# Half of the channel products of an attention-and-mixing kernel end by ScalarE's maximum with zero and an adding transfer by GpSimd

## The chip, the cores and the metric

The kernel runs on one core of a Trainium2 chip. The metric is the device time of one execution in microseconds (us), from the program's start to its end; the median of several runs is compared. The engines are named as in the profile: PE is TensorE, PEld its weight loads, DVE is VectorE, ACT is ScalarE, POOL is GpSimd and SP is SyncE, which issues transfers.

## The reference

Eight batches, each with eight heads, 576 positions and a head size of 64. Attention keeps only the scores within `tau` of the row's maximum; its output is laid out as `x` (576 by 512 for each batch) and goes through a mixing layer:

```python
scores = scale * q @ k.T
scores = where(scores >= max(scores) - tau, scores, -1e9)
x = softmax(scores) @ v                       # heads side by side: 576 x 512
theta = x @ w_theta
y = w_tok_r @ (x * cos(theta)) + w_tok_i @ (x * sin(theta))
u = x + y
out = u + maximum(u @ w_ch, 0)
```

## The kernel before

Work goes in 32 pairs of heads (four pairs a batch). A pair has five units. A unit's scores are matmuls (L761) into PSUM banks. DVE reads them out with a running minimum of the negated scores, which is the maximum (L782, tile `sc`), ACT takes the exponential (L815, tile `s`), and DVE zeroes what lies under the threshold and sums the row (L822). The weights are then turned: in three pairs of four by DVE's transpose (L837), in the last pair of each batch by PE (L855), with ACT copying each turned block out of PSUM (L861, L873, tile `a`). The product with the values is L891, or L920 in the pairs turned by PE. ACT copies it into the tile `xT`, which holds one pair's 128 channels of `x` in fp32 as 128 by 576, and it is divided by the row sums (L969 on POOL, L975 on DVE).

Every fp32 operand of a matmul is split into a high part, rounded by ACT (L982 for `x`, L708 for `q`, L722 for `k`), and a low part, which is a subtraction on POOL or DVE (`low`, L539). Matmuls of 128 by 128 weights on 288 columns then build the products from three terms.

`mixture(b)` does the mixing layer of one batch while the attention of the next one runs. For each of four blocks of 128 channels `m` it makes the angle product (L1021; ACT writes the tile `ang` at L1041 and L1055), sines, the turned parts `zh` and `zl`, and the token product (L1209), which DVE adds onto `xT` at L1221. Then `xT` holds `u`. `parts_of` splits `u`, and the channel product of block `m` (again L1021, from weights `wm` that SP loads at L680) fills two banks, one for each half `h` of 288 columns. `evict` (L1255) ends it: one DVE instruction for each half takes the maximum with zero of the bank, adds `u` and writes onto `xT` (L1270). SP then stores `xT` (L1278).

The tile class `ang` has two buffers and `xT` has seven. A table of numbers, `ORDER`, names every operation of the program in the order in which it is issued, and so sets each engine's queue; `PLACES` names the buffer of each tile. Engines work through their queues in order, and a waiting instruction holds back those behind it. SP's transfers are in the same way in order of issue.

`evict` of before holds a second way, not taken there since `rc` and `rc0` are 0: for `m` under `rc`, and for all batches but the last, ACT writes the maximum into an `ang` tile and POOL adds it onto `xT`.

Of the kernel before, what the change touches and what calls it, by code (L numbers as in the profile page):

```python
# [79 lines left out]
        "4456744475625423500000040000004000044607650506740743067473236547236454575624376627535473625473"  # L80
# [45 lines left out]
        "0101010101010101010101010101010101010101010101010101010101010101"  # L126
    ),
    "zh4": (
        "0123012301230123012301230123012301230123012301230123012301230123"
    ),  # L130
    "zl4": (
        "0123012301230123012301230123012301230123012301230123012301230123"
# [296 lines left out]
def tile_attn_moe(  # L429
# [98 lines left out]
    def gps(occ, fn, key, R, W, lock=True):  # L528
        return op(POOL, occ, fn, key, R, W, tail=0.05, lock=lock)
# [856 lines left out]
```

## Time and profile before

| | |
|---|---|
| time, median of 3 runs | 952.08 us (949.31 to 953.31) |
| the profiled execution's own time | 950.14 us |
| its span, first to last instruction | 948.3 us |
| outside the span | 1.8 us |
| granted TensorE clock, mean over the span | 0.994 of full speed |

The profile is of one execution. Busy time of an engine is the time in which one of its instructions ran; a matmul's end is modelled, so that a busy PE may still hold short gaps. A line such as `A <- B` in the waits says that the engine of A sat idle until B had ended. "issue" stands for idle time with no releaser in the profile.

### The profile page before, as it was taken

The page shows a single profiled execution, that of the slowest core. Times are in us where ns is not written, and L with a number is a line of the kernel's source. Part 1 is how long each engine was busy: PE and PEld are TensorE (multiplying, and loading weights), DVE is VectorE, ACT ScalarE, POOL GpSimd, SP SyncE. Part 2 cuts the span into 40 slices and gives each one's busy share as a digit, 9 for nine tenths or more (in the row PEclk, how much of TensorE's full clock was granted, in tenths as well). Part 3 has the DMA queues.
Part 4 walks back from the last instruction along what each step waited for, and adds up shares of the span by engine and source line. Part 5 has one row for each costly group of instructions (what it writes and reads, how often), then busy time and mean ns, then how long its engine had stood idle before and what let it go on. Part 6 is the DMA issues. An engine that isn't in the chain of part 4 may idle for free.

```text
span 948.3 us, 30033 instructions
## 1 busy us (share of the span) xinstructions
PE 904.9 (95%) x12532; PEld 801.8 (85%) x12532; DVE 796.5 (84%) x1838; ACT 634.1 (67%) x1296; POOL 342.8 (36%) x390
## 2 busy tenths in 40 slices
PE   6889999999999999999899999999999999999998
PEld 5667788898898889888798988898898988899798
DVE  7999899979988988889798897879998798986342
ACT  7899997458945777467764767548784578635650
POOL 2234453125624345234432533432442353404110
PEclk9999999999999999999999999999999999999999
DMA  6366253435322353325403453044533153222322
GB/s 219 125 195 199 85 184 125 142 123 192 122 86 92 116 178 120 127 78 179 147 37 104 136 192 112 4 172 122 192 99 112 55 196 123 70 97 98 114 70 73
DMA packets 59288, 118.80 MB, mean 125 GB/s; under 512 B 19441, under 2 KB 28561, under 8 KB 56593
## 3 DMA queue, kind: packets, MB, share of 16 engines
q1 hardware_dynamic: 59008, 116.89, 37.2%
q8 instruction: 98, 1.61, 0.7%
q14 instruction: 38, 0.30, 0.1%
q10 hardware_dynamic: 144, 0.00, 0.0%
HBM read 103.09 MB, written 13.78 MB: 123 GB/s over the span
## 4 chain that ended last, share of the span: by engine, by line
PE 60%; DVE 22%; ACT 10%; issue 5%; POOL 2%; DMA 0%; SPq 0%; DVEq 0%; ACTq 0%; POOLq 0%
PE banks_ps__66 L1209 19%; PE banks_ps__66 L1021 12%; PE banks_ps__66 L761 10%; PE banks_ps__66 L891 9%; DVE sc L782 6%; DVE s L822 6%; PE banks_ps__66 L855 4%; DVE a L837 4%; PE banks_ps__66 L1164 3%; PE banks_ps__66 L920 2%; ACT s L815 2%; POOL z L1139 1%; DVE xl L539 1%; DVE z L1089 1%; ACT L1117 1%
## 5 line engine op out<-in xcount | busy, mean ns | idle before, releaser
L815 ACT ACTIVATE s<-sc,nm 128x576 f32<-128x576 f32 x288 | 219.5, 777 | 73.0 <-DVE sc L782 57.3
L822 DVE SCALAR_TENSOR_TENSOR s<-sc,nm,s 128x576 f32<-128x576 f32 x288 | 249.7, 888 | 14.9 <-ACT s L815 7.9
L782 DVE TENSOR_SCALAR_CACHE_REDUCE sc<-banks_ps__66 128x576 f32<-128x576 f32 x261 | 188.3, 744 | 23.0 <-PE banks_ps__66 L761 21.7
L761 PE MATMUL banks_ps__66<-k,q 64*128 64x288 f32 (+1 forms) x1728 | 173.9, 313 | 12.9 <-DVE sc L782 7.9
L1021 PE MATMUL banks_ps__66<-xh,wm 128*128 128x288 f32 x1024 | 170.9, 304 | 2.2 <-issue 1.6
L761 PEld LDWEIGHTS banks_ps__66<-k,q 64*128 64x128 f32 (+1 forms) x1728 | 137.9, 189 | 39.8 <-issue 15.2
L1209 PE MATMUL banks_ps__66<-wt_h,zh 128*128 128x288 f32 x576 | 159.1, 303 | 1.3 <-ACT zh L1170 0.4
L1209 PE MATMUL banks_ps__66<-wt_l,zh 128*128 128x288 f32 x576 | 158.0, 299 | 0.0
L1021 PEld LDWEIGHTS banks_ps__66<-xh,wm 128*128 128x128 f32 x1024 | 144.8, 190 | 9.5 <-issue 6.2
L1139 POOL TENSOR_TENSOR z<-z,xT 128x288 f32<-128x288 f32 x112 | 98.7, 914 | 128.6 <-ACT z L1120 118.0
L837 DVE STREAM_TRANSPOSE a<-s 128x576 f32<-128x576 f32 x160 | 117.4, 757 | 20.6 <-PE banks_ps__66 L891 18.6
L539 POOL TENSOR_TENSOR xl<-xT,xh 128x288 fp32r<-128x288 f32 x78 | 75.3, 987 | 141.8 <-ACT xh L982 120.5
L891 PE MATMUL banks_ps__66<-a,v 32*64 32x144 f32 x5760 | 105.9, 286 | 12.9 <-issue 11.0
L1209 PEld LDWEIGHTS banks_ps__66<-wt_h,zh 128*128 128x128 f32 x576 | 106.8, 188 | 7.0 <-issue 4.1
L891 PEld LDWEIGHTS banks_ps__66<-a,v 32*64 32x64 f32 x5760 | 91.5, 130 | 23.5 <-issue 18.9
L1209 PEld LDWEIGHTS banks_ps__66<-wt_l,zh 128*128 128x128 f32 x576 | 107.3, 188 | 2.0 <-issue 1.9
L539 POOL TENSOR_TENSOR k<-rawk,k 128x288 fp32r<-128x288 f32 x62 | 57.9, 942 | 113.7 <-ACT k L722 78.1
L1209 PE MATMUL banks_ps__66<-wt_h,zl 128*128 128x288 f32 x576 | 98.7, 299 | 0.0
L539 POOL TENSOR_TENSOR q<-rawq,q 128x320 fp32r<-128x320 f32 x56 | 57.8, 1045 | 111.8 <-ACT q L708 111.8
L1021 PE MATMUL banks_ps__66<-xl,wm 128*128 128x288 f32 x512 | 92.6, 301 | 0.9 <-DVE xl L539 0.6
L1209 PEld LDWEIGHTS banks_ps__66<-wt_h,zl 128*128 128x128 f32 x576 | 82.8, 188 | 1.4 <-issue 1.2
L855 PE MATMUL banks_ps__66<-ident,s 128*128 128x128 f32 (+1 forms) x492 | 74.8, 284 | 3.1 <-DVE s L822 2.1
(84 smaller groups left out, 1275.0 us busy)
## 6 DMA issues: line engine op xcount, KB each, us to landing
wm<-wm_dram SPq DMA_DIRECT2D x64, 512.0 KB
v<-in_vp_dram SPq DMA_DIRECT2D x20, 1152.0 KB
rawq<-in_qT_dram SPq DMA_DIRECT2D x31, 320.0 KB
rawk<-in_kT_dram SPq DMA_DIRECT2D x31, 288.0 KB
out_dram<-xT SPq DMA_DIRECT2D x31, 288.0 KB
rb<-sums_dram SPq DMA_DIRECT2D x64, 128.0 KB
v<-in_vp_dram SPq DMA_DIRECT2D x12, 576.0 KB
z<-in_w_tok_dram SPq DMA_DIRECT2D x9, 576.0 KB
```

The source lines that it names most:

```text
L539: eng.tensor_tensor(out=out()[:, c0:c1], in0=in0()[:, c0:c1], in1=in1()[:, c0:c1], op=ALU.subtract)
L761: nc.tensor.matmul(ps()[:, 2 * j + h, :HS], q[a]()[r, i * P : (i + 1) * P], k[c]()[r, h * HS : (h + 1) * HS], start=(x == 0), stop=(x == 2),)
L782: lambda j=j, sc=sc, scaled=scaled: nc.vector.tensor_scalar(out=sc().rearrange("p (a b) -> p a b", a=2), in0=ps()[:, 2 * j : 2 * j + 2, :H ...
L815: lambda j=j, sc=sc, weights=weights: nc.scalar.activation(out=weights(), in_=keys(sc()), func=AF.Exp, bias=nm()[:, j : j + 1], scale=-1.0),
L822: lambda j=j, sc=sc, total=total, weights=weights: nc.vector.scalar_tensor_tensor(out=weights(), in0=keys(sc()), scalar=nm()[:, 2 + j : 3 ...
L837: nc.vector.transpose(out=a()[:, :, j, 32 * i : 32 * i + 32], in_=src.rearrange("p (c q) -> p c q", q=32))
L855: nc.tensor.transpose(out=tp()[: k1 - k0, c * P : (c + 1) * P], in_=flat()[:, k0:k1], identity=ident)
L891: nc.tensor.matmul(ps()[64 * h : 64 * h + 64, b, :w], v()[r, c, h, :], a()[r, c, h, :], start=(c == 0), stop=(c == 17))
L1021: nc.tensor.matmul(ps[h]()[:, :HS], wm()[:, a, c, :], parts[c][bb]()[:, h * HS : (h + 1) * HS], start=first and n == 0, stop=final and n = ...
L1139: eng.tensor_tensor(out=zi, in0=zi, in1=x[m]()[:, c0:c1], op=ALU.mult)
L1164: nc.tensor.transpose(out=tp()[:, i * P : (i + 1) * P], in_=z()[:, c : c + P], identity=ident)
L1209: nc.tensor.matmul(ps()[:, :HS], zz[c][lo]()[:, zz[c][2]], w[:, c, hs], start=(q + n == 0), stop=(q + n == len(work) - 1),)
```

## The change

For blocks `m` = 0 and 1 of batches 0 to 6 (`rc` and `rc0` are now 2), that is for 14 of the 32 channel products, the second way of `evict` is taken, with another last step. ACT writes the maximum with zero of each half into an `ang` tile (two instructions a block, 28 in all, L1269 of the kernel after). After the second half one transfer issued by GpSimd adds the tile of 128 by 576 onto `xT` in SBUF (`add_to`, 14 in all, L538). The 28 DVE instructions of L1270 for these blocks are gone; 36 stay. The store of `xT` by SP waits for the transfer's landing.

`low` gets a parameter `by_dma` that no caller sets. `ORDER` is a new table throughout, and the buffers of `zh4`, `zl4` and `ang` follow it.

```diff
-    "pad_pe": 0.12, "pad_dve": 0.021, "pad_act": 0.148, "rc": 0, "za": 0, "zq": 0, "ab0": 0, "rc0": 0, "za0": 0, "zq0": 0,
+    "pad_pe": 0.12, "pad_dve": 0.021, "pad_act": 0.148, "rc": 2, "za": 0, "zq": 0, "ab0": 0, "rc0": 2, "za0": 0, "zq0": 0,
...
 ORDER = (
-    "176 3 -9 3 75 -71 -176 177 2 -153 144 10 -9 79 -251 183 -169 160 -134 135 -122 131 146 -145 2 -1 3 8 -9 -186 "
...
+    "179 -3 -6 3 -172 26 150 71 -77 9 -8 -158 164 3 -181 174 9 68 -198 122 9 146 -290 145 2 -1 3 8 -9 -186 188 -187 "
...
+    def add_to(out, src, key, R, W, kb):
+        o = gps(0.87, lambda: nc.gpsimd.dma_start(out=out(), in_=src(), accum_op=ALU.add), key, R, W, lock=False)
+        o.kb = 1.2 * kb
+
...
                         c_act(HS, True), lambda: nc.scalar.activation(out=part()[:, hs], in_=ps()[:, :HS], func=AF.Relu), key,
                         (ps,), ((part, h),),
                     )
-                    gps(
-                        c_pool(HS),
-                        lambda: nc.gpsimd.tensor_tensor(out=x[m]()[:, hs], in0=part()[:, hs], in1=x[m]()[:, hs], op=ALU.add),
-                        key, ((part, h), x[m]), ((x[m], [0, 1, ("h", h)]),),
-                    )
+                    if h:
+                        add_to(lambda: x[m](), lambda: part(), key, (part, x[m]), ((x[m], [0, 1, ("h", 0), ("h", 1)]),), 288)
                     return
```

Where the program's queues changed is shown at one place, the channel products of batch 4. Line numbers of the kernel after are higher: L1277 there is L1270 of before, L792 is L782, L832 is L822, L825 is L815, L871 is L861, L803 is L793, L544 is L539, L979 is L969, L709 is L699, L731 is L721, L690 is L680, L747 is L737, L960 is L950 and L1285 is L1278.

DVE, before, from the first end of block 0 to the second end of block 1 (`s_` and a number is one unit's weights):

```order
L1270 SCALAR_TENSOR_TENSOR xT<-banks_ps__66,xT 128x288
L822 SCALAR_TENSOR_TENSOR s_9834,rows<-sc,nm,s_9834 128x9x64
L1270 SCALAR_TENSOR_TENSOR xT<-banks_ps__66,xT 128x288
L782 TENSOR_SCALAR sc,nm<-banks_ps__66 128x576 x2
L822 SCALAR_TENSOR_TENSOR s_9834,rows<-sc,nm,s_9834 128x9x64
L782 TENSOR_SCALAR sc,nm<-banks_ps__66 128x576
L822 SCALAR_TENSOR_TENSOR s_9882,rows<-sc,nm,s_9882 128x9x64 x2
L822 SCALAR_TENSOR_TENSOR s_9921,rows<-sc,nm,s_9921 128x576
L1270 SCALAR_TENSOR_TENSOR xT<-banks_ps__66,xT 128x288
```

DVE, after, the same units (9834 and 9882 are now called 9852 and 9893):

```order
L832 SCALAR_TENSOR_TENSOR s_9852,rows<-sc,nm,s_9852 128x9x64
L792 TENSOR_SCALAR sc,nm<-banks_ps__66 128x576 x2
L832 SCALAR_TENSOR_TENSOR s_9852,rows<-sc,nm,s_9852 128x9x64
L792 TENSOR_SCALAR sc,nm<-banks_ps__66 128x576
L832 SCALAR_TENSOR_TENSOR s_9893,rows<-sc,nm,s_9893 128x9x64 x2
L832 SCALAR_TENSOR_TENSOR s_9929,rows<-sc,nm,s_9929 128x576
```

The ends of the blocks have left the queue, and what stood between them is in the same order as before.

ACT, before, the same stretch:

```order
L815 ACTIVATE s_9834<-sc,nm 128x9x64
L861 COPY a<-banks_ps__66 128x4x128
L815 ACTIVATE s_9882<-sc,nm 128x9x64
L861 COPY a<-banks_ps__66 128x4x128
L815 ACTIVATE s_9882<-sc,nm 128x9x64
L793 ACTIVATE nm<-nm,small 128x2
```

ACT, after:

```order
L825 ACTIVATE s_9852<-sc,nm 128x9x64
L1269 ACTIVATE ang<-banks_ps__66 128x288
L825 ACTIVATE s_9893<-sc,nm 128x9x64
L1269 ACTIVATE ang<-banks_ps__66 128x288
L871 COPY a<-banks_ps__66 128x4x128
L803 ACTIVATE nm<-nm,small 128x2
L825 ACTIVATE s_9893<-sc,nm 128x9x64
```

The two maxima of block 0 now stand between the exponentials; one copy (L861) has moved behind them and the small L793 ahead of the last exponential, and no work has left the stretch.

SP, after, from the store of block 0 (the first row) to that of block 1 (the last):

```order
L1285 DMA out_dram<-xT 128x576
L747 DMA v<-in_vp_dram 128x2304
L731 DMA rawk<-in_kT_dram 128x576
L690 DMA wm<-wm_dram 128x1024 x2
L747 DMA v<-in_vp_dram 128x2304
L960 DMA sums_dram<-rt 9x128
L709 DMA rawq<-in_qT_dram 128x640
L1285 DMA out_dram<-xT 128x576
```

Behind each store, which now waits for an adding transfer, stand loads of the next pairs.

## Rows read from the trace of the kernel before

**Rows 1.** Page, part 1: busy us of each engine (share of the span), instructions.

```profile
PE 904.9 (95%) x12532; PEld 801.8 (85%) x12532; DVE 796.5 (84%) x1838; ACT 634.1 (67%) x1296; POOL 342.8 (36%) x390
```

**Rows 2.** Busy us of each engine by stage; first the stage and its length.

```profile
0.00:75.00 75.00, 59.39 (x495) 44.08 (x495) 68.92 (x180) 63.09 (x132) 21.01 (x34) 0.95 0.58 182
75.00:875.00 800.00, 777.16 (x11492) 692.79 (x11491) 699.72 (x1607) 543.10 (x1111) 312.47 (x344) 1.00 0.37 123
875.00:948.30 73.30, 68.37 (x550) 64.97 (x549) 27.82 (x52) 27.95 (x55) 9.34 (x12) 1.00 0.26 90
```

**Rows 3.** Waits of PE from 75 to 875 us: us in total, times, longest.

```profile
PE banks_ps__66 L891 <- issue: 11.0, 9, 2.0
...
PE banks_ps__66 L761 <- DVE sc L782: 1.3, 4, 0.4
PE banks_ps__66 L855 <- DVE s L822: 1.1, 4, 0.3
```

**Rows 4.** Groups by line and form: busy us, mean ns of one, idle before.

```profile
L1270 DVE SCALAR_TENSOR_TENSOR xT<-banks_ps__66,xT 128x288 f32<-128x288 f32 x64 | 27.9, 450 | 16.8 <-PE banks_ps__66 L1021 13.9 <-PE banks_ps__66 L855 2.0 <-ACT xh L982 0.5
...
L1041 ACT ACTIVATE ang<-banks_ps__66 128x288 f32<-128x288 f32 x64 | 25.8, 415 | 12.7 <-PE banks_ps__66 L1021 7.3 <-DVE z L1089 5.1 <-PE banks_ps__66 L946 0.2
```

**Rows 5.** Stages (columns PE, PEld, DVE, ACT, POOL) around blocks 0 and 1.

```profile
199.00:205.00 6.00, 6.00 (x135) 5.29 (x135) 2.73 (x7) 2.11 (x7) 0.00 (x0) 1.00 0.48 162
312.60:322.00 9.40, 9.40 (x86) 8.71 (x84) 8.65 (x23) 8.79 (x21) 2.90 (x4) 1.00 0.60 184
421.00:432.00 11.00, 11.00 (x101) 9.99 (x100) 9.46 (x29) 10.80 (x25) 3.32 (x5) 1.00 0.35 103
533.00:542.00 9.00, 9.00 (x81) 8.44 (x78) 8.62 (x26) 8.46 (x20) 2.41 (x3) 1.00 0.59 198
644.50:657.00 12.50, 12.50 (x112) 11.45 (x111) 11.65 (x35) 12.17 (x29) 4.87 (x6) 1.00 0.34 89
756.40:766.20 9.80, 9.80 (x86) 8.93 (x86) 8.80 (x27) 9.69 (x25) 4.84 (x6) 1.00 0.42 145
867.80:874.00 6.20, 6.20 (x52) 6.18 (x51) 4.32 (x14) 3.22 (x9) 0.00 (x0) 1.00 0.66 224
...
sum 51.70, PE 51.70 PEld 47.52 DVE 47.17 ACT 49.91 POOL 18.34; mean PE 10.34 PEld 9.50 DVE 9.43 ACT 9.98 POOL 3.67
```

**Rows 6.** Sum of the stages 322:338, 432:450, 542:558, 657:672 and 766.2:782.

```profile
sum 80.80, PE 80.35 PEld 66.29 DVE 77.93 ACT 52.30 POOL 34.48; mean PE 16.07 PEld 13.26 DVE 15.59 ACT 10.46 POOL 6.90
```

**Rows 7.** DVE's instructions of L1270 in one stage: length, busy us, count.

```profile
644.50:657.00 12.50, 1.81 (x4) 1.00 0.34 89
```

**Rows 8.** Chain of waits from 644 to 672 us: start, length, what.

```profile
653.21 0.79 ACT s L815
...
655.13 0.68 ACT s L815
...
657.83 0.69 ACT s L815
...
661.47 0.37 DVE xT L1270
```

**Rows 9.** Instructions of L539: ns least/median/most, first and last start.

```profile
L539 POOL TENSOR_TENSOR xl<-xT,xh x78: 794/812/1397, 110.6 to 932.3; 128x288 fp32r<-128x288 f32 x78
...
L539 DVE TENSOR_TENSOR xl<-xT,xh x25: 708/986/1421, 112.8 to 933.5; 128x576 fp32r<-128x576 f32 x25
```

**Rows 10.** Waits of SP's queue: us in total, times, longest.

```profile
SPq L1278 <- DVE xT L1270: 37.3, 11, 9.7
...
SPq L958 <- DMA sums_dram<-rt: 24.7, 18, 3.9
```

**Rows 11.** Issues of the stores by SP: ns least/median/most of one issue.

```profile
L1278 SPq DMA_DIRECT2D out_dram<-xT x31: 332/382/1504, 199.9 to 942.8; - x31
```

More of the change, by code (lines that the diff above doesn't have):

```diff
@@ L79 @@
         "60074446576565447457764665756457746577456700000040000007000074504570505640664055006744567564574676564765"
-        "4456744475625423500000040000004000044607650506740743067473236547236454575624376627535473625473"
+        "4456744475625423500000040000004000044607650506740743067473236547236454575624373627535473625473"
     ),
@@ L125 @@
     "ang": (
-        "0101010101010101010101010101010101010101010101010101010101010101"
+        "010101010101010101010101010101010101010101010101010101010101010101010101010101"
     ),
     "zh4": (
-        "0123012301230123012301230123012301230123012301230123012301230123"
+        "0123012301230123012301230123012301230123012301230123012301230112"
     ),
     "zl4": (
-        "0123012301230123012301230123012301230123012301230123012301230123"
+        "0123012301230123012301230123012301230123012301230123013201230121"
     ),
@@ L534, in load, with low @@
         return o
-    def low(on_pool, out, in0, in1, key, R, W, n=S):
+    def add_to(out, src, key, R, W, kb):
+        o = gps(0.87, lambda: nc.gpsimd.dma_start(out=out(), in_=src(), accum_op=ALU.add), key, R, W, lock=False)
+        o.kb = 1.2 * kb
+    def low(on_pool, out, in0, in1, key, R, W, n=S, by_dma=False):
         def go(eng, c0=0, c1=n):
@@ L541, in low @@
         (b, p), k = W, AT["cut"]
+        if on_pool and by_dma:
+            both = (b, [(p, i) for i in range(k)])
+            act(c_act(n), lambda: nc.scalar.activation(out=out(), in_=in0(), func=AF.Copy, scale=-1.0), key, R[:1], (both,))
+            add_to(lambda: out().bitcast(F32), in0, key, R[:1], (both,), n // 2)
+            return
         if on_pool:
```

321 rows, old and new, of the table ORDER are left out of this document.

## The prediction

> **What bounds the kernel now.** I read the page's busy times first. PE is busy for 904.9 of 948.3 us, DVE for 796.5, ACT for 634.1 [rows 1]. The view by stage then splits the span: in the first 75 us PE is idle for 15.6 us, in the 800 us from 75 to 875 for 22.8 us, and in the last 73 us, where DVE has little left, for 4.9 us [rows 2]. So the middle is PE's, to 97%. Who ends PE's idle time there: half of it (11.0 us) has no releaser and lies in the products with the values, and each wait for DVE is about 1 us in total [rows 3]. DVE is busy for 87% of the middle, close behind PE, and has to be looked at by stretch.
>
> The change touches 28 places, four a batch in batches 0 to 6. I laid a window around the four of each batch, from the end of the first half of block 0 to that of the last half of block 1 [rows 5]; in batch 0 the last of the four comes later. The reader is to see three things. PE is busy for every hundredth of a microsecond in all seven. In batches 1 to 5 both other engines are packed: of 51.70 us DVE works 47.17 and ACT 49.91, so ACT, not DVE, is the fuller one. In batches 0 and 6 DVE and ACT both have gaps. The reason for ACT's load is in the code: these are the units of the pair that PE turns and whose turned blocks ACT copies. In the windows right behind (80.80 us in five batches) it is the other way round: DVE works 77.93 us, ACT only 52.30, and PE 80.35 [rows 6].
>
> **The change part by part.**
>
> Removed from DVE: 28 instructions of 450 ns [rows 4], 12.6 us. Batches 0 and 6 hold 8 of them, in windows with DVE idle: worth nothing. The other 20 are 9.0 us, 1.8 us a batch (batch 4 is shown in [rows 7]). PE has no idle time beside them, so PE's work covers them; what can be won is that DVE goes into its packed second window 1.8 us earlier.
>
> Added to ACT: 28 instructions. The nearest row is the same engine reading the same 288 columns of a bank into `ang`, 415 ns [rows 4]: 11.6 us in all, 1.66 us a batch. In the five full windows ACT's gaps are 51.70 - 49.91 = 1.79 us, 0.36 us a batch. So 1.3 us of ACT's work a batch is pushed into the second window, which has 28.5 us of ACT's time free. Until then exponentials and copies run up to 1.3 us late, and behind them wait DVE's L822 and then PE's transposes. In batch 4 the chain runs just there through ACT's exponentials, and from 658.5 us on through DVE [rows 8].
>
> The two together: from above, ACT is on the path each time and nothing is given back, 5 x 1.66 = +8.3 us. From below, DVE's head start goes through each time, -9.0 us. I take 0, for two reasons: PE, which covers both windows, has 0.45 us of idle time in 132.5 us [rows 5, 6], and ACT gives back in the second window what it lost in the first.
>
> Added to POOL: 14 issues. No row shows an issue by POOL. The nearest from below is an issue by SP, 0.38 us at the median [rows 11], from above the longest POOL subtraction, 1.40 us [rows 9]: 5 to 20 us on an engine that is busy for 36% of the span. POOL's idle time covers it, 33.4 us of the 51.7 [rows 5], and I cost it at nothing; without that cover it would come onto the splits of `x`, `q` and `k`. An issue also might hold up a DVE instruction. DVE's own subtraction L539 takes 708 ns at best, 986 at the median and 1421 at worst, while POOL works beside it with a spread of 794 to 1397 [rows 9]. 14 x 0.28 is 3.9 us, 14 x 0.71 is 9.9 us, and none is zero; I take zero, as an issue reads and writes far fewer bytes than such a subtraction and is nearer to SP's issues.
>
> The Trainium skill, "SBUF — State Buffer", section "SBUF: two separate sides", speaks against the change: a transfer issued by GpSimd has its descriptors written by GpSimd, which is locked out of SBUF while DVE runs in a mode that uses both ports, so that the transfer lands late. The rows above do show DVE and POOL getting in each other's way; no row here shows it for an issue. The page tells of a transfer of 0.62 us that took 3.1 us beside such an instruction; 2.5 us more would leave the landing below within what SP bears, so by that rule the sum would stay, and it is the third rival that hangs on it.
>
> The adding transfer itself: 295 KB are read twice and written once. No row has one. In the window at 867.8 us all transfers together move 224 GB/s [rows 5]; one pass of 295 KB at that rate is 1.3 us, two are 2.6 us, and twice that when the windows' transfers share the rate: 2.6 to 5.3 us, estimates. The longest wait for the landing of a small transfer (9 by 128 row sums) was 3.9 us [rows 10]. I take 4 to 6 us. What waits for it is the store on SP, and behind that the loads of `v`, `rawk` and `wm`. SP already stands up to 9.7 us at the stores, 37.3 us in total [rows 10], while PE loses nothing to loads in the middle. So this is covered up to about 10 us. The `ang` tile is needed again only by the next batch's angles, behind blocks 2 and 3.
>
> The new order: the whole table is new, and queues differ slightly far from the 28 places too. What a new order can give back is PE's idle time, at most 22.8 us in the middle [rows 2]; what it can cost has no such bound. There is no reason in the rows for either sign. I take 0 and a width of 6 us.
>
> **Sum.** 950.14 us of the profiled execution (span 948.3 and 1.8 around it) - 0 + 0 = 950.1 us. This execution lies 1.9 us under the median of 952.08 and inside its runs (949.31 to 953.31), so the same sum from the median is 952.1. I say **951 us**: no change that a measurement here can tell, since about 0.5% (4.8 us) is needed for that, under 947.3 or over 956.8 us.
>
> **The rivals.**
>
> 1. DVE's head start counts, faster. For it: DVE is 96% busy in the second windows [rows 6], and in batch 4 the chain from 658.5 us on is DVE's [rows 8]; ACT has room there, and a new order can use that. Against it: PE is busy throughout. The price is between half and all of the 9.0 us: 950.1 - 4.5 to - 9.0, 941 to 945.6 us.
>
> 2. ACT takes DVE's place, slower. The place is the five full windows: exponentials late by the four maxima, then L822, then the transposes and PE's product with the values. For it: ACT's 97% there against DVE's 91% [rows 5], and the rows of ACT's queue, where the maxima stand between exponentials. Against it: PE has other work queued. It decides as soon as PE runs dry in the 80 us behind, that is when its idle time there is no longer 0.45 us [rows 6]. Full price 950.1 + 8.3 = 958.4 us.
>
> 3. The adding transfer lands late (DVE keeps POOL from its descriptors, or the transfer is slow), slower. It decides from a landing of about 10 us, the wait that SP bears now [rows 10]; at 15 us SP would be 5 us behind 14 times, and if one time in seven a load were late by that, 2 x 5 = 10 us: 960 us. Against it: transfers use 37% of their engines in the middle [rows 2].
>
> 4. The change doesn't do what it says: DVE's work only moves and the 9 us reappear as longer L822 beside POOL's issues. That is 950 us too, and counts with the forecast.
>
> **How the numbers follow.** Forecast with rival 4: 0.46, its own range 945 to 957, of which 0.05 falls under 947.3 and 0.04 over 956.8. Rival 1: 0.28, with 0.26 under 947.3. Rival 2: 0.18, of which 0.02 stays within the bound. Rival 3: 0.08. Faster is 0.05 + 0.26 = 0.31; within the bound 0.37 + 0.02 + 0.02 = 0.41; slower 0.04 + 0.16 + 0.08 = 0.28. The range that leaves out a tenth on each side goes from the middle of rival 1 to rival 2 and part of rival 3: 942 to 961 us.
>
> **What would show it.** In the profile after: L1270's successor 36 times instead of 64, DVE's busy time down by about 12 us, ACT's up by about 11.6 us with a new group of 28 at about 415 ns, and PE's busy time about as before (905 us). If the forecast holds, PE's idle time from 75 to 875 us is 18 to 28 us. Rival 1 shows as PE idle time under 18 us with waits of ACT for DVE (`sc`) shorter. Rival 2 shows as new waits of DVE for ACT's exponentials, or of PE for ACT's copies. Rival 3 shows as waits of SP for the adding transfer over 10 us, and POOL or PE behind loads. I am wrong if the time is outside 947 to 957 us, and wrong in the mechanism if PE's idle time moves by over 6 us while the time does not.

## The result and the profile after

The kernel after takes 959.46 us (median of 4 runs, 957.51 to 960.52), before in the same comparison 951.71 us: a ratio of 1.0100, interval 1.0075 to 1.0124. (The two medians alone give 1.0081, 7.75 us; the ratio on record is a little higher, and the medians' value lies inside its interval.) It is slower, against a forecast of no change. The profiled execution took 957.51 us, its span is 955.7 us, its mean granted clock 0.993. Line numbers are those of the order rows above: L832 is L822 of before, and so on.

Part 1 of the page of the kernel after, busy us of each engine, answers to [rows 1]:

```profile
PE 907.2 (95%) x12532; PEld 803.0 (84%) x12532; DVE 795.9 (83%) x1810; ACT 640.8 (67%) x1324; POOL 356.6 (37%) x404
```

DVE has 28 instructions fewer, but is busy for only 0.6 us less, where 12.6 us were taken from it. The stages answer to [rows 2] (columns PE, PEld, DVE, ACT, POOL, clock, DMA share, GB/s):

```profile
0.00:75.00 75.00, 59.94 (x490) 43.91 (x490) 68.01 (x178) 62.09 (x129) 19.85 (x34) 0.95 0.58 181
75.00:875.00 800.00, 772.04 (x11441) 687.49 (x11442) 697.52 (x1575) 545.66 (x1128) 325.20 (x356) 1.00 0.40 126
875.00:955.70 80.70, 75.23 (x603) 71.57 (x602) 30.34 (x60) 33.06 (x69) 11.59 (x14) 1.00 0.34 107
```

PE's idle time in the middle went from 22.8 to 28.0 us, and the last stage is 7.4 us longer: attention reaches 875 us with more work left. PE's waits in the middle answer to [rows 3] (us in total, times, longest):

```profile
PE banks_ps__66 L901 <- issue: 11.3, 7, 2.9
PE banks_ps__66 L771 <- DVE sc L792: 4.3, 8, 1.4
PE banks_ps__66 L865 <- DVE s L832: 2.1, 3, 1.6
PE banks_ps__66 L1174 <- POOL z L1149: 1.9, 2, 1.7
PE banks_ps__66 L956 <- DVE rows L952: 1.9, 4, 1.3
PE banks_ps__66 L1031 <- DVE xT L1277: 1.4, 1, 1.4
```

What has no releaser is the same in total, 11.3 against 11.0 us, in fewer and longer pieces; the two longest, 2.94 and 2.68 us, end at 610 and 799 us. Waits for DVE have grown. The groups that the change touches (busy us, mean ns, idle before) answer to [rows 4], and the transfers' issues and landings (least, median, most), shown nowhere before, follow:

```profile
L1277 DVE SCALAR_TENSOR_TENSOR xT<-banks_ps__66,xT 128x288 f32<-128x288 f32 x36 | 15.3, 444 | 14.2 <-PE banks_ps__66 L1031 14.2
L1269 ACT ACTIVATE ang<-banks_ps__66 128x288 f32<-128x288 f32 x28 | 11.5, 413 | 6.0 <-PE banks_ps__66 L1031 5.7
```

```profile
L538 POOL DMA_DIRECT2D xT<-ang x14: 837/870/1018, 199.7 to 888.2; - x14
DMA to landing us min/median/max: 3.5/4.8/9.4
```

The new wait of SP's queue, beside [rows 10]:

```profile
SPq L1285 <- DMA xT<-ang: 45.7, 8, 9.1
```

Finally the timeline where the kernel after falls back most, with DVE's L832 and all of POOL (start, us, and in brackets the idle time before):

```profile
755.65 0.81 DVE L832 SCALAR_TENSOR_TENSOR s<-sc,nm,s 128x576 f32<-128x576 f32 x1
756.07 0.87 POOL L538 DMA_DIRECT2D xT<-ang  x1 [9.12 <-issue]
756.39 3.51 DVE L832 SCALAR_TENSOR_TENSOR s<-sc,nm,s 128x576 f32<-128x576 f32 x1
756.68 2.60 POOL L979 TENSOR_TENSOR xT<-xT,rb 128x288 f32<-128x288 f32 x3
759.84 0.81 DVE L832 SCALAR_TENSOR_TENSOR s<-sc,nm,s 128x576 f32<-128x576 f32 x1
```

An L832 of 0.81 us lasts 3.51 us: it begins during POOL's issue of the adding transfer and ends 0.62 us after the last of three POOL instructions that follow it. Another lasts 3.00 us at 768 us, behind the next transfer.

### The profile page after: what moved, and what is told of

It is laid out like the page before. It is cut to its first block, busy times and chain, and to the rows that moved or that the text cites. A ratio compares the mean times of both kernels' runs of the same rounds, so it can differ in the third digit from the quotient of the medians.

```text
span 955.7 us, 30075 instructions
## 1 busy us (share of the span) xinstructions
PE 907.2 (95%) x12532; PEld 803.0 (84%) x12532; DVE 795.9 (83%) x1810; ACT 640.8 (67%) x1324; POOL 356.6 (37%) x404
## 4 chain that ended last, share of the span: by engine, by line
PE 58%; DVE 25%; ACT 8%; issue 6%; POOL 2%; DMA 0%; SPq 0%; DVEq 0%; ACTq 0%; POOLq 0%
PE banks_ps__66 L1219 19%; PE banks_ps__66 L1031 12%; PE banks_ps__66 L901 9%; PE banks_ps__66 L771 9%; DVE sc L792 8%; DVE s L832 7%; DVE a L847 5%; PE banks_ps__66 L865 4%; PE banks_ps__66 L1174 3%; ACT s L825 2%; POOL z L1149 1%; PE banks_ps__66 L930 1%; PE banks_ps__66 L651 1%; ACT a L871 1%; DVE zl L1199 1%
## 5 line engine op out<-in xcount | busy, mean ns | idle before, releaser
L832 DVE SCALAR_TENSOR_TENSOR s<-sc,nm,s 128x576 f32<-128x576 f32 x288 | 256.1, 911 | 25.4 <-ACT nm L803 14.4
L825 ACT ACTIVATE s<-sc,nm 128x576 f32<-128x576 f32 x288 | 217.9, 777 | 70.7 <-DVE sc L792 60.2
L792 DVE TENSOR_SCALAR_CACHE_REDUCE sc<-banks_ps__66 128x576 f32<-128x576 f32 x261 | 188.7, 745 | 25.4 <-PE banks_ps__66 L771 19.5
L544 POOL TENSOR_TENSOR xl<-xT,xh 128x288 fp32r<-128x288 f32 x78 | 80.3, 1056 | 108.4 <-ACT xh L992 92.1
L901 PE MATMUL banks_ps__66<-a,v 32*64 32x144 f32 x5760 | 106.1, 286 | 12.3 <-issue 11.3
L544 POOL TENSOR_TENSOR q<-rawq,q 128x320 fp32r<-128x320 f32 x56 | 57.9, 1050 | 111.1 <-ACT q L718 96.3
L544 POOL TENSOR_TENSOR k<-rawk,k 128x288 fp32r<-128x288 f32 x62 | 58.4, 950 | 96.3 <-ACT k L732 82.4
```

Of the source, the lines that this page charges most:

```text
L544: eng.tensor_tensor(out=out()[:, c0:c1], in0=in0()[:, c0:c1], in1=in1()[:, c0:c1], op=ALU.subtract)
L792: lambda j=j, sc=sc, scaled=scaled: nc.vector.tensor_scalar(out=sc().rearrange("p (a b) -> p a b", a=2), in0=ps()[:, 2 * j : 2 * j + 2, :H ...
L825: lambda j=j, sc=sc, weights=weights: nc.scalar.activation(out=weights(), in_=keys(sc()), func=AF.Exp, bias=nm()[:, j : j + 1], scale=-1.0),
L832: lambda j=j, sc=sc, total=total, weights=weights: nc.vector.scalar_tensor_tensor(out=weights(), in0=keys(sc()), scalar=nm()[:, 2 + j : 3 ...
L901: nc.tensor.matmul(ps()[64 * h : 64 * h + 64, b, :w], v()[r, c, h, :], a()[r, c, h, :], start=(c == 0), stop=(c == 17))
```

## The experiments

Ratios are to the kernel before on the same chip. "Over before" is (ratio - 1) times 950 us, in us. e4 and e5 leave out the adding transfers, so that their output lacks the maximum in these blocks.

| run | ratio, 95% interval | over before |
|---|---|---|
| the kernel after itself | 1.0100 (1.0075 to 1.0124) | 9.5 |
| e1 new order, DVE ends | 1.0063 (1.0043 to 1.0084) | 6.0 |
| e2 old order, adding transfers | 1.0150 (1.0122 to 1.0178) | 14.3 |
| e3 after, two transfers later | 1.0074 (1.0049 to 1.0098) | 7.0 |
| e4 after, no transfers | 1.0062 (1.0042 to 1.0083) | 5.9 |
| e5 old order, no transfers | 1.0011 (0.9988 to 1.0035) | 1.0 |
| e6 old order, transfers behind runs | 1.0098 (1.0061 to 1.0136) | 9.3 |
| e7 old order, POOL additions | 1.0020 (1.0001 to 1.0039) | 1.9 |
| e8 old head, new tail, DVE ends | 1.0074 (1.0045 to 1.0102) | 7.0 |
| e9 as e1, three SP entries later | 1.0147 (1.0123 to 1.0170) | 14.0 |
| e10 after, repaired as e3 and e9 | 1.0148 (1.0125 to 1.0170) | 14.1 |
| e11 new head, old tail | 1.0014 (0.9994 to 1.0035) | 1.3 |
| e12 before, idle POOL transfers | 1.0016 (1.0000 to 1.0033) | 1.5 |
| e13 as e1, two loads later | 1.0031 (1.0010 to 1.0052) | 2.9 |
| e14 as e3, two loads later | 1.0057 (1.0035 to 1.0078) | 5.4 |
| e15 as e6, stores later | 1.0292 (1.0260 to 1.0324) | 27.7 |
| e16 as e13, two PE moves | 1.0072 (1.0053 to 1.0090) | 6.8 |
| e17 as e14, two PE moves | 1.0058 (1.0032 to 1.0084) | 5.5 |

**The change taken apart: table against ends (e1 to e5).** The old order with the new ends (e2) has each transfer's issue right behind the second maximum.

```diff
 e1, on after:           "rc": 2, "rc0": 2  ->  "rc": 0, "rc0": 0    (new ORDER without the 14 transfers)
 e2, on before:          rc 0 -> 2, evict and add_to of after        (old ORDER)
 e3, on after, POOL:     transfer of block 0, batch 5, behind three L979; of block 1 behind the next two
 e4, on after, e5, on e2:
-        nc.gpsimd.dma_start(out=out(), in_=src(), accum_op=ALU.add)
+        None
```

e1: 

> The kernel after with its new ORDER, but the ends of blocks 0 and 1 again on DVE (28 instructions of 450 ns, 12.6 us), in the places where ACT's maxima stood; no adding transfers. Theory A (the adding transfers cost the 7.75 us: a transfer that waits in GpSimd's queue holds back ready GpSimd work, which then runs in one piece and keeps DVE's L832 waiting, 3.51 and 3.00 us at 756 and 768): 947 to 953 us, as the new table alone is level or a few us ahead (the scores ran 5.5 us ahead of before at 598 us). Theory B (the new table itself is the slower one): 958 to 964 us. Theory C (DVE's 12.6 us were worth their time, and the add cost more than that): 955 to 958 us would need both.

e2: 

> The kernel before with its own ORDER; only the 28 DVE ends of blocks 0 and 1 are changed to ACT's maximum, and each adding transfer is issued by GpSimd right behind the second maximum. Theory A (adding transfers): 956 to 963 us. Theory B (the new table): 948 to 953 us, no change against before.

e3: 

> The kernel after, with the two adding transfers of batch 5 moved back in GpSimd's queue, the first behind the three L979 that ran in one piece after it, the second behind the next two instructions of GpSimd. Theory A: the 3.51 and 3.00 us L832 fall under 1.6 us, and the time falls by 3 to 5 us, to 954 to 956.5 us. Theory B, and any theory in which these two long L832 are a symptom of lateness: 958 to 960 us.

e4: 

> The kernel after without the 14 adding transfers: ACT still writes the maxima, DVE is still relieved, nothing adds them, so the output lacks the maximum in these blocks. Theory A: 946 to 952 us, since all that is left of the change helps DVE by 12.6 us. Theory B: 957 to 960 us, the transfers being innocent.

e5: 

> The kernel before with its own ORDER and ACT's maxima in place of the 28 DVE ends, but without the adding transfers, so the output lacks the maximum in blocks 0 and 1 of batches 0 to 6. Theory D (what costs 15 us in the old order is a GpSimd transfer issue straight ahead of a run of GpSimd tensor instructions: DVE's instruction is then held until the run's end, 4.26, 3.75, 2.40, 4.49 and 2.97 us long in five places): no DVE instruction over 1.6 us, and the time within 3 us of before. Rival E (ACT's 28 maxima delay the exponentials, and that costs the 15 us): 10 us or more over before.

Both of my first theories were half right. The new table alone costs 6.0 us (e1), and the transfers cost much in the old order: 14.3 us (e2) against 1.0 without them (e5). DVE's relief is worth nothing in either table: e5 is level with before, e4 with e1. Theory A's repair (e3) removed the two long L832 of batch 5, but its time cannot be told from that of after. Two things are then to be explained, the transfers and the table.

**What a GpSimd transfer does to DVE (e2, e5, e6, e7, e12).** e2 has the queues of before, so that each operation's delay against before can be read one by one. It grows in steps, 5 us at 215, 2 at 330, 4 to 5 at 550. At each of these a DVE instruction is held. The timeline of e2 with DVE's L834 (L822 of before) and POOL:

```profile
550.30 0.87 POOL L540 DMA_DIRECT2D xT<-ang  x1 [1.25 <-DMA rb<-sums_dram]
550.39 4.49 DVE L834 SCALAR_TENSOR_TENSOR s<-sc,nm,s 128x576 f32<-128x576 f32 x1 [1.28 <-ACT nm L805]
550.91 1.85 POOL L981 TENSOR_TENSOR xT<-xT,rb 128x288 f32<-128x288 f32 x2
552.44 1.82 POOL L546 TENSOR_TENSOR k<-rawk,k 128x288 fp32r<-128x288 f32 x2
```

At 214.53 us it is a small one; at this place of before the same instruction takes 515 ns, at 537 us of after 169 ns:

```profile
213.93 0.88 POOL L540 DMA_DIRECT2D xT<-ang  x1 [3.11 <-ACT a L873]
214.53 4.26 DVE L953 TENSOR_SCALAR rows<-rows 128x9 f32<-128x9 f32 x1
219.18 0.37 PE L958 MATMUL banks_ps__66<-ident,rows 128*9 128x128 f32 x1 [3.45 <-DVE rows L954]
```

PE waits 3.45 us behind it, and at 219 us its granted clock falls from 1.00 to 0.50 (from the 2.4 to the 1.2 GHz level) for 3.4 us, another 1.7 us. Two of the five holds (214 and 550 us) have such a fall behind them. Three variants then ask what makes a hold:

```diff
 e6, on e2, POOL queue: five of the transfers go behind the run of tensor instructions ahead of which they stood
   (in SP's queue stores of these blocks go behind them)
 e7, on before: "rc": 0 -> 2 alone; its own second way, at the same places
+                        nc.gpsimd.tensor_tensor(out=x[m]()[:, hs], in0=part()[:, hs], in1=x[m]()[:, hs], op=ALU.add)
 e12, on before, behind DVE's second end of blocks 0 and 1:
+        nc.gpsimd.dma_start(out=idle_dram[b, m], in_=x[m]())
```

e6: 

> The kernel before with its own ORDER and ACT's maxima, all 14 adding transfers kept; five of them (one in each of batches 0, 1, 2, 3 and 5) are moved behind the run of GpSimd tensor instructions ahead of which they stood, and two stores of SP behind them. Theory D: the five held DVE instructions are gone, and with them 12 to 14 us of the 16; time 0 to 4 us over before. Rival F (the holding comes from the transfer's own traffic into SBUF or its landing, which follows wherever it stands): the time stays 12 us or more over before.

e7: 

> The kernel before with its own ORDER and its own second way: ACT's maxima, and 28 GpSimd tensor additions (each at the place behind its maximum) in place of the 14 transfers. GpSimd waits in the same places, and has 28 more instructions in its runs, some 0.75 us each, but issues no transfer. Theory D: no DVE instruction over 1.7 us; time 2 to 8 us over before, for the longer runs alone. Rival G (it is the waiting in GpSimd's queue, that piles up its work, and not the transfer's issue): DVE instructions of 3 to 5 us as before, and 15 us or more.

e12: 

> The kernel before, its own ORDER, all ends on DVE; added are 14 plain transfers issued by GpSimd behind the second end of blocks 0 and 1 (the finished block of 128 by 576 to a scratch place in DRAM), at the places in GpSimd's queue where the old order with adding transfers had them. Nothing waits for them. Theory D (a transfer's issue by GpSimd straight ahead of a run of its tensor instructions keeps DVE out until the run's end, whatever the transfer does): DVE instructions of 2.4 to 4.5 us in three to five places, and 5 to 13 us over before. If it takes the accumulation, or a read and write of SBUF by the transfer: no DVE instruction over 1.6 us, and under 2 us over before.

The line of L822 by its lengths (least, median, most) in before, e2, e6, e7 and e12:

```profile
L822 DVE SCALAR_TENSOR_TENSOR s<-sc,nm,s x288: 757/814/1522, 8.9 to 871.0; 128x576 f32<-128x576 f32 x144
```

```profile
L834 DVE SCALAR_TENSOR_TENSOR s<-sc,nm,s x288: 757/815/4493, 8.8 to 884.5; 128x576 f32<-128x576 f32 x144
```

```profile
L834 DVE SCALAR_TENSOR_TENSOR s<-sc,nm,s x288: 758/815/1535, 8.9 to 880.3; 128x576 f32<-128x576 f32 x144
```

```profile
L825 DVE SCALAR_TENSOR_TENSOR s<-sc,nm,s x288: 758/814/1468, 8.7 to 874.1; 128x576 f32<-128x576 f32 x144
```

```profile
L826 DVE SCALAR_TENSOR_TENSOR s<-sc,nm,s x288: 758/815/3370, 8.9 to 869.7; 128x576 f32<-128x576 f32 x144
```

e7 decides against the waiting in POOL's queue: it waits in the same places and has 28 more tensor instructions (24.4 us), and no DVE instruction is held. e12 decides against the accumulation: plain transfers that nothing waits for hold DVE for 3.37, 2.03 and 1.63 us. It costs only 1.5 us, where I expected 5 to 13. Its three holds add 4.6 us to the usual 0.81 us of that line, e2's five add some 14 us. A hold also need not cost its length where PE has other work, which it had not at 215 us of e2; this second reason is argued, not shown. e6 shows that the place makes it: with the transfers behind the runs the holds are gone, and DVE is busy for 785.2 us instead of e2's 796.9. No kernel here without GpSimd transfers has a DVE instruction over 1.6 us; e2 has five, and after has four (3.51, 3.00, 1.78 and 1.71 us).

But e6 gave back only 5 of the 12 to 14 us that I expected (9.3 against 14.3 us, by ratios whose intervals overlap). The rest looked like SP's: its wait for the landings (total, times, longest), and PE's wait for `wm`, which before does not have:

```profile
SPq L1287 <- DMA xT<-ang: 71.6, 10, 14.4
```

```profile
PE banks_ps__66 L1033 <- DMA wm<-wm_dram: 5.1, 4, 2.6
```

```diff
 e15, on e6, SP queue: each of the 14 waiting stores goes behind the next four transfers
```

e15: 

> The old order with ACT's maxima and the adding transfers behind the runs of GpSimd work (9.1 us over before in its earlier run), with each of the 14 stores that wait for an adding transfer moved back in SP's queue by four transfers (fewer where a store of row sums would be passed). Theory V (the rest of the cost is SP: it stands at these stores for 71.6 us in all, the loads behind come late, PE waits 5.1 us for wm and 1.9 us for v, and the clock falls twice, 1.7 us each): SP's wait falls under 40 us, PE's waits for wm and v under 2 us, and the time is 1 to 4 us over before. Otherwise it stays 7 us or more over.

It failed. SP's wait for landings fell to 3.5 us and PE waits for no load any more, but each store frees an `xT` buffer, so that ACT's copies into the next tile came late (PE waits 11.0 us for ACT's L919), and the time rose. e6's last 9 us are not separated further, and that they are SP's is not shown.

**What the new table costs (e8 to e11, e13, e14, e16, e17).** With DVE ends the new table (e1) is level with before up to 782 us and 6.4 us late at 869, counted by the starts of L782, the first with the first and so on. The two tables have issued the same set of operations at their 3435th (about 689 us) and 3885th place (about 777 us), so they can be joined there.

```diff
 e8, ORDER:      before up to 3885, new table behind, all ends on DVE
 e11, ORDER:     new table with transfers (batches 0 to 4) up to 3435, before behind
```

e8: 

> All ends on DVE, no transfers. ORDER is that of before in its first 3885 operations (up to about 777 us) and the new table behind. If what the new table loses by itself lies in its last part, as the trace with the new table and DVE ends shows (level at 782 us, 6.4 us late at 869): 5 to 8 us over before. If it is spread over the whole, or hangs on the new head: under 3 us over before.

e11: 

> The new table with ACT's maxima and adding transfers in batches 0 to 4 (10 of 14) up to its 3435th operation, some 689 us, and behind it the table of before with the ends of batches 5 and 6 on DVE. The trace after was 2.5 to 3 us ahead of before there. If that lead is real and the loss is all behind it: 946 to 949 us where before is 950 (faster by 0.1 to 0.4%). If the lead is a matter of one run, or is given back whatever follows: 949 to 952 us.

The new tail alone costs the whole 6 to 7 us. The lead of the new head, 3 us in the trace of after, did not come through (e11): no version here beats before. The granted clock of every run is on record, and the mean over e11's runs is 0.991 against 0.996 for before; over 952 us that is some 4 us (an estimate, the span times the difference), as much as the lead. In the tail the first thing to see is at 794 us: the stages of before, of after (two), of e1 (two) and of e13, columns as above:

```profile
794.00:798.00 4.00, 2.74 (x83) 2.27 (x71) 3.35 (x8) 3.97 (x6) 2.26 (x2) 1.00 0.18 44
```

```profile
794.00:798.00 4.00, 2.12 (x132) 1.86 (x116) 4.00 (x9) 3.97 (x6) 1.95 (x3) 1.00 1.00 273
798.00:802.00 4.00, 3.19 (x23) 2.81 (x23) 0.60 (x2) 1.08 (x1) 4.00 (x5) 0.60 0.46 145
```

```profile
794.00:798.00 4.00, 0.86 (x43) 0.60 (x31) 3.11 (x6) 3.56 (x5) 3.46 (x4) 0.82 0.92 277
798.00:802.00 4.00, 4.00 (x26) 3.62 (x21) 0.00 (x0) 0.00 (x0) 3.52 (x5) 0.50 0.19 74
```

```profile
794.00:798.00 4.00, 3.07 (x31) 2.87 (x31) 2.15 (x3) 2.82 (x5) 4.00 (x5) 1.00 0.03 5
```

PE is in its 192 small matmuls of one product with the values. In the new table two loads of `wm` of 512 KB and a store of 288 KB run beside them: the transfers' engines are 92 to 100% busy, PE stands still for 2.7 (after) to 3.1 us (e1) with no releaser, and its clock then falls to 0.50. In before it stands still for 1.26 us and the clock stays. SP's queue in after around it, and PE's piece behind the wait:

```profile
793.07 0.32 SPq L690 DMA_DIRECT2D wm<-wm_dram  x1
793.45 0.42 SPq L1285 DMA_DIRECT2D out_dram<-xT  x1
...
796.41 1.27 SPq L690 DMA_DIRECT2D wm<-wm_dram  x1
```

```profile
798.80 0.78 PE L901 MATMUL banks_ps__66<-a,v 32*64 32x144 f32 x13 [2.68 <-issue]
```

What PE waits for stands in the trace too. Part 3 of the page of after lists a transfer queue of the kind `instruction` (packets, MB, share of the transfer engines); in the trace's records of single packets each of the 98 is 16 KiB:

```profile
q8 instruction: 98, 1.61, 0.7%
```

In the 19 traces of this case PE stands still 160 times for more than 0.7 us with no releaser, from 75 us on. All 160 pieces end 1.2 to 1.8 us (median 1.4) after such a packet has ended, though the packets come about 10 us apart. So PE waits there for its next block of instructions. At 794 us the packet takes 0.9 us in before, after and e1 alike; what differs is its start. In before it starts 1.10 us before PE runs dry, in after 0.29 us and in e1 0.82 us after that.

```diff
 SP queue, e13 (on e1), e14 (on e3); e9 and e10 move the store too:
-wm<-wm_dram
 out_dram<-xT
 rb<-sums_dram ...
-wm<-wm_dram
 v<-in_vp_dram
+wm<-wm_dram
+wm<-wm_dram
 PE queue, e16 (on e13), e17 (on e14): a score product (838 us) behind two more pieces of the token product,
 the row sums' turning (844 us) behind two pieces of the product with the values
```

e9: 

> The new table with all ends on DVE (957.4 us, 7.9 over before, in its earlier run), with three entries of SP's queue moved: the two 512 KB loads of wm that were issued at 791.6 and 794.9 us and the 288 KB store at 792.0 stand behind the next load of v (806.9 us); the products that read those two loads come only at some 865 us. Theory T (these 1.3 MB run beside PE's 192 small matmuls at 791 to 798 us, PE then stands still for 2.6 to 3.3 us there with no releaser, and its granted clock falls to 0.5 of full speed for some 4 us): the still time falls to 1.6 us or less, the clock stays at 1.00 from 790 to 810, and the time falls by 3 to 5 us, to 3 to 5 us over before. Theory U (the loss of the new table's last part is in its order of DVE and PE work around 840 to 855, and covers whatever is won at 795): under 1.5 us are won.

e10: 

> The kernel after with both repairs: batch 5's two adding transfers behind the GpSimd work that they stood ahead of, and the same three entries of SP's queue moved as in the run before this one. By theory T 953 to 956 us where before is 950 (after was 7.75 over before, the late transfers alone 7.0 over): 3 to 5 us over before. By theory U 6 to 8 us over before.

e13: 

> The new table with all ends on DVE, and only the two 512 KB loads of wm (issued at 791.6 and 794.9 us) moved behind the next load of v; the store at 792.0 us stays, since its move held ACT for 9.3 us in the run with three entries moved (ACT's copy into the reused xT buffer waited for that store), while PE's still time at 794 had fallen from 3.32 to 1.72 us and the clock had stayed at 1.00. Theory T: the still time at 794 us is under 2 us, no fall of the clock before 810 us, no 6.8 us wait of PE at 805, and 2.5 to 5 us less than the unmoved table, that is 2 to 5 us over before. Theory U (the DVE and PE order around 840 to 870 covers it): 5.5 to 8 us over before.

e14: 

> The kernel after with batch 5's two adding transfers behind the GpSimd work that they stood ahead of, and the two loads of wm moved as in the run before this one, the store left where it was. Theory T: 2.5 to 5.5 us over before. Theory U: 6 to 8 us over before.

e16: 

> The new table with all ends on DVE and the two loads of wm moved (3.2 us over before in its earlier run), with two more moves on PE's queue where it stood still for 1.43 us at 838 us (a score product waiting for DVE to free a bank) and 1.45 us at 844 us (the turning of the row sums, waiting for DVE's reciprocals): the score product stands behind two more pieces of the token product, the turning of the row sums behind two pieces of the product with the values. Theory W (what is left of the new table's loss are such places in PE's queue): both waits go, 1.5 to 3 us are won, 0.2 to 1.7 us over before. Rival X (DVE is the bound there, 24.4 of 25 us busy at 825 to 850 us, so PE waits elsewhere for it): less than 1 us is won.

e17: 

> The kernel after with all repairs: the two late adding transfers of batch 5, the two loads of wm, and the two moves in PE's queue. Theory W: 2.4 to 4 us over before (4.8 to 5.4 less the 1.5 to 3), what is left over the kernel with DVE's ends being the adding transfers themselves, some 2 us. Rival X: 4.5 us or more over before.

In e9 the still time fell from 3.14 to 1.54 us and the clock stayed there, but the moved store frees the buffer that ACT's next copy needs, and ACT, DVE and PE all stopped; e10 did the same. ACT's copy in e9:

```profile
810.99 0.59 ACT L916 COPY xT<-banks_ps__66 128x512 f32<-128x512 f32 x1 [9.31 <-DMA out_dram<-xT]
```

With the two loads alone (e13) the stage above is clean: the instruction packet starts 1.27 us before PE runs dry, the still time is 1.27 us, and the table's cost falls from 6.0 to 2.9 us, with intervals that overlap a little. On the kernel after (e14 against e3) it falls from 7.0 to 5.4 us, with intervals that overlap. What is left of the table is not in two places of PE's queue: e16 removed the two waits and got a wait of 1.9 us for the same engine, DVE, a little later. It is 3.9 us slower than e13, not faster, and e17 equals e14. That speaks for DVE's work in that stretch as its bound, but does not show it; which order of it costs the time, and why e16 lost, is left open.

The new table has a second collision of the same kind, in its head, and no run here moved it. Loads of `rawq`, `rawk` and `wm`, issued by SP at 603 to 604 us of after, run beside the small matmuls of the product with the values. The stages of before and of after in which PE runs dry, and PE's piece of after behind the wait:

```profile
612.00:616.00 4.00, 2.83 (x121) 2.36 (x104) 2.22 (x6) 0.58 (x2) 0.00 (x0) 1.00 0.04 8
```

```profile
604.00:608.00 4.00, 3.02 (x176) 2.73 (x176) 2.91 (x7) 0.87 (x2) 0.00 (x0) 1.00 0.84 283
```

```profile
609.96 0.52 PE L901 MATMUL banks_ps__66<-a,v 32*64 32x144 f32 x17 [2.94 <-issue]
```

PE waits there for the 63rd instruction packet. In all eleven traces with the new head it stands still for 2.9 to 4.2 us, the packet starts 0.6 to 1.9 us after PE ran dry, and the clock falls to 0.50. In the eight traces with the old head the piece before the same packet's instructions is 1.3 us at most, and no fall follows. In e13 it is 2.95 us and a fall that costs 1.7, against 1.17 us and none in before: 3.5 us, an estimate, where 2.9 us are left of the table's cost. Whether moving these loads too would win them is not tested.

## Why the prediction was wrong

The forecast fails at one step of the sum, "The new order: ... I take 0 and a width of 6 us". Its size was off: the table alone is worth +6.0 us (4.1 to 8.0, e1), all behind 777 us (e8), and some 3 us of it are two loads that collide with PE's small matmuls (e13). What failed there in the mechanism: the loads delay PE's next instructions, PE stands still, and its clock falls behind that. The rows could not give this number, but they held the sign of danger: half of PE's idle time was in those very products with no releaser [rows 3], and I did not ask which transfers the new table puts beside them. The sum has no term for the clock either. The mean granted clock of after's four runs is 0.9905, that of before's runs in the experiments 0.9944 to 0.9957; over 956 us that is 3.7 to 5.0 us (an estimate, the span times the difference), about half of the loss. It is not a cause beside the others, since the falls follow PE's still times, though not every still time has one.

The second failed step is the price of POOL's issues, "I take zero, as an issue reads and writes far fewer bytes". The reason was wrong: what held DVE were the tensor instructions behind the issue (e6), whatever its own bytes, which no run measured. In the old order DVE is busy for 11.1 us more than without transfers (796.9 in e2, 785.8 in e5), above my upper bound of 9.9 us. In the kernel after the table avoids most of this: with the transfers DVE works 3.4 us more (795.9 against 792.5 in e4). DVE's busy time adds up: 796.5 us before, +5.3 by the new table (801.8 in e1), -9.3 by the maxima on ACT (792.5 in e4), +3.4 by the transfers. What the transfers cost in time in the new table is not resolved: after against e1 it is 3.5 us by the ratios, whose intervals overlap a little, and nothing by the medians (7.75 and 7.87 us over before); e14 against e13, on one chip, gives 2.5 us with intervals that overlap.

The exchange of DVE's ends for ACT's maxima was right, at zero: e5 against before, e4 against e1. ACT's 28 instructions took 413 ns (415 forecast; its busy time rose by 6.7 us, not 11.6), and PE's idle time in the middle, 28.0 us, lies at the edge of the 18 to 28 foretold. The landing was right at the median, 4.8 us, with 9.4 at worst; SP's cover holds in the new table, where PE waits for no load, and not in the old one, where it waits 5.1 us for `wm` in e6.

Rival 4 named a part of what happened to DVE's time (the transfers' 3.4 us; the table's 5.3 it did not name), but took it to be free. Rival 3 did not come true: the transfers landed within 9.4 us of their issue in after and within 6.2 us in e2 and e6. Its sign alone shows in the old order, where SP waits up to 14.4 us; over 8 us of that wait lie ahead of the issue. And POOL kept DVE out, not DVE POOL. Rival 2's waits for ACT did not appear. Rival 1 fails with e5.

On the holds: the Trainium skill, "SBUF — State Buffer", section "SBUF: two separate sides", says that the port pair which DVE and GpSimd share is locked by whichever instruction starts first, for the whole of that instruction. By that, DVE would wait for one POOL instruction, and a POOL subtraction of `x` lasts 1.40 us at most in before [rows 9]. Before and e7 agree (no L822 over 1.52 us); behind a transfer's issue the measurement differs: DVE waited for a run of four (4.49 us).

On the still time: the Trainium skill, "Runtime: NRT & Kernel Launch", section "Instruction fetch mechanics", says that an engine's sequencer fetches instructions in blocks by a DMA queue of its own. The traces agree: PE's long pieces without a releaser end 1.2 to 1.8 us behind a packet of queue q8. That loads beside it make the packet start late is shown by e13, where moving two loads brought its start from 0.82 us behind PE's stop to 1.27 us ahead of it. Why it starts late beside them, no run here shows.

## What to carry to other kernels

A change that comes with a rewritten order is two changes: run the order with the old operations first, and the new operations in the old order. A transfer issued by GpSimd should stand behind a run of its tensor instructions, not ahead of one, where DVE is near its bound (e6 has none of e2's holds). Where PE stands still with no releaser, look in the trace at the packets of the instruction queue, and at the loads beside them. Before an entry of a transfer queue is moved, look at what its end frees: three times here a store moved later stopped the engine that waited for its buffer.

## What was not expected of the hardware

- After a GpSimd transfer's issue (0.54 to 1.02 us), GpSimd's tensor instructions can run through without letting DVE in: holds of 2.4 to 4.5 us behind five of e2's 14 transfers, on an instruction of 128 by 9 too, and of 1.6 to 3.4 us behind three of e12's. Without transfers DVE got its turn within 1.52 us in before.
- PE's next block of instructions comes by a transfer queue, and loads beside it delay it: PE stood still for 2.7 to 3.1 us at 799 us of after and e1 and for 1.27 us with two loads moved (e13).
- The falls of PE's granted clock to 0.50 lasted 3.4 us (1.7 us lost) in most places here, and 6.8 or 10.2 us in a few. PE had stood still for 1.22 us before one (e2, 344 us) and for 3.45 us before another (e2, 215 us). The longest still time of before [rows 3], 2.0 us at 465 us, has none behind it in its profile; the same piece has one in e5's. e13 and e16 have the same queues up to 830 us, and in their profiled executions e16 has one fall more (at 577 us): such chance is as large as some of the differences sought here.
- 28 GpSimd additions of 873 ns (e7) cost less than 14 adding transfers in the same places (e2): 1.9 against 14.3 us.
